# A second product made of seven, for the last 1024 tokens of a chunk-attention and ELU-FFN kernel

## The chip, the cores and the metric

The program runs on one core of one Trainium2 chip. The metric is device time in microseconds (us). The engines are TensorE (PE; its weight loads are listed apart as PEld), VectorE (DVE), ScalarE (ACT), GpSimd (POOL) and SyncE (SP), which issues the DMA transfers. The kernel before took 849.08 us, the median of three runs (848.92 to 850.63).

## The reference

```python
# q, k, v: 8 batches, 8 heads, 576 tokens, 64 features; chunks of 64 tokens
scores = 1/sqrt(64) * q_c @ k_c^T             # inside one chunk of 64 tokens
attn = exp(scores - max) ; attn = attn / (sum(attn) + 1e-9)
x = (attn @ v_c) -> 4608 tokens x 512         # heads side by side
h = x @ w_in                                  # 512 x 2048
g = where(h > 0, h, exp(min(h, 0)) - 1)       # ELU
out = g @ w_out                               # 2048 x 512, float32
```

The weights come as 64-bit floats, the rest as 32-bit floats.

## The kernel before

**Numbers.** Every operand of a large product is kept as a pair `hi`, `lo` of the rounded type float32r, whose sum is the float32 value. `three` (L405) makes one product of 128 x 128 by 128 x 512 from three matmuls: hi by hi, hi by lo, lo by hi. A split is a rounding copy on ACT (`hi`) and a subtraction on DVE or POOL (`lo`).

**Blocks.** The 4608 tokens are 9 blocks of 512. Three blocks are plain: for each of 16 slices f of the 2048 hidden features `hidden(f)` makes the slice of h from 4 `three`, `elu` and a split follow, and the slice goes into a queue of second products. The other six blocks form three superblocks of 1024 tokens (s = 0, 1, 2). There the first product is made by Winograd's form of Strassen's scheme: with weights and tokens cut in halves, a pair of slices (g = 0 to 7) for both token halves needs seven products of halves instead of eight. Their weight operands, among them four sums (S1 to S4), are made once, in the second plain block, by `combine` (L469: sums on POOL, split on ACT and DVE, written to `a_dram`), and loaded for each pair (`load_a`, 256 KB each, L531). The token operands T1 to T4 are made by `prepare` (L560). x_ps and y_ps are the two PSUM banks in which the products p1 to p7 add up; c1 to c4 (`keep`, L628) copy x_ps away on ACT, and d1 to d3 (`add`, L631) add y_ps to such a copy on DVE.

**Second product.** In all blocks before the change it is plain: `second_next` (L644) takes one item from the queue and makes one `three` of 128 tokens by 512 output columns, with w_out as the moving operand. 16 slices add up in four PSUM banks (o0 to o3), one for each 128 tokens. Results are copied to SBUF and stored in rows of 2 KB (`copy_out`, L446). The lo parts of w_out are loaded from `lo_dram` in a ring (`load_lo`, 512 KB for two slices, L546).

**Order.** PE, ACT, DVE and SP follow the source exactly; the order inside a block is written out in strings, one word for one step. POOL's order is chosen by the framework. One superblock is eight passes through PAIR and then the 16 lines of KEPT: in PAIR the first 512 tokens' h is used at once, while the other 512 tokens' is kept in `g_kept` and multiplied in KEPT. The words that matter here:

- p1 to p7, c1 to c4, d1 to d3 as above; Q is one item of the second product (three matmuls);
- 1, 2, 3, 4 are the next step of the pair's four ELU parts (1 and 3 end in a split and an entry in the queue, 2 and 4 in `g_kept`); 5 is 3 of the pair before;
- m, E, z, h, s, v, x, q, k, l, V are the attention of the tokens needed next: l issues eight q and k loads of 128 KB (sixteen of 64 KB where the 128 tokens lie in two batches), h ends with a DVE transpose, the ACT copy `unturned` (L369) and four small transfers `turned` on SP (L373), which the product v in the same pair needs;
- in KEPT, G splits the next kept slice.

As SP works in the order of the source, one pair's list on SP is: the weight load for p1 of the next pair after p1, then p2, p6, the four `turned` transfers, p5, the q and k loads, p7, p4, p3, and the v load; the lo load of w_out falls among the last.

Of the kernel before, what the change touches and what calls it, by code (L numbers as in the profile page):

```python
# [10 lines left out]
F32 = mybir.dt.float32  # L11
# [9 lines left out]
def kernel(  # L21
# [26 lines left out]
    P = 128  # L48
# [17 lines left out]

    first = ctx.enter_context(tc.tile_pool(name="first", bufs=1))
    sm = ctx.enter_context(tc.tile_pool(name="sm", bufs=4))
    stp = ctx.enter_context(tc.tile_pool(name="stp", bufs=3))
    fill = ctx.enter_context(tc.tile_pool(name="fill", bufs=1))  # L70
    const = ctx.enter_context(tc.tile_pool(name="const", bufs=1))
# [4 lines left out]
    ident = first.tile([P, P], F32, name="ident")  # L76
    fill.tile([P, 64], F32, name="unused")
    k_turned = const.tile([P, NK, P], F32, name="k_turned")
# [445 lines left out]
    def flat(t):  # L524
        return t.rearrange("p a b -> p (a b)")

    def a_place(i: int):

        return flat(weights[0][0])[:, i * 4 * P:(i + 1) * 4 * P]
# [114 lines left out]
    def second_next():  # L644
        if not queue:
            return
        (n0, o_ps, put), f, tt, hi, lo = queue.pop(0)
        ts = slice(tt * P, (tt + 1) * P)
# [8 lines left out]
        if not plain and tt == NTT - 1 and f % 2:  # L657
            uses.append(f)
            if len(uses) + RING <= NG * (1 + 2 * NS):
                load_lo((f - 1 + 2 * RING) % NF)  # L660

    RING = NG // 2
# [49 lines left out]
    def warm(n: int):  # L712
# [53 lines left out]
    SECOND_PAIR = (  # L766
        "p1 c1 5 5 h Q 4 p2 d1 4 Q q k p6 c2 1 Q Q 1 p5 1 1 Q l p7 c3 d2 Q Q 2 p4 c4 2 Q 3 p3 d3 "
        "3 3 3 s v x V"
    )
    PAIR = (  # L770
        "m p1 c1 4 E Q 4 z p2 d1 Q p6 c2 h 1 Q Q 1 p5 1 q k 1 Q l p7 c3 d2 Q Q 2 p4 c4 2 Q 3 p3 d3 "
        "3 3 3 s v x V"
    )
    KEPT = (
# [186 lines left out]
    def do(item: str):  # L961
        if item == "Q":
            second_next()
        elif item == "P":
            second_products()
# [32 lines left out]
    t3_place.append(late.tile([P, 2, 2 * TB], F32R, name="t3_place"))  # L998
    c11, c21 = [late.tile([P, TB], F32, name=name) for name in ("c11", "c21")]
    x_ps, y_ps = [ps_h.tile([P, TB], F32, name="h") for _ in range(2)]  # L1000

    pair = None
    for s in range(NS):
        n0 = (PLAIN + 2 * s) * TB
        run = n0, o_tiles(), a_half_place
        for g in range(NG):
            before, pair = pair, Pair(s * NG + g)
            for item in ((FIRST_PAIR, SECOND_PAIR)[g] if not s and g < 2 else PAIR).split():
                if item[0] == "p":
                    pair.product(int(item[1]))  # L1010
                elif item[0] == "c":
                    pair.keep(int(item[1]))
                elif item[0] == "d":
                    pair.add(int(item[1]))
                elif item in "45":
                    if before:
                        next(before.parts["3" if item == "5" else item], None)
                elif item in "123":
                    next(pair.parts[item])
                else:  # L1020
                    do(item)
        preparing, kept = s + 1 < NS, iter(range(NF))
        run = n0 + TB, o_tiles(), b_half_place
        for line in KEPT:
            for item in line.split():
                if item == "4":
                    next(pair.parts["4"], None)
                elif item == "G":
                    split_kept(next(kept))
                else:  # L1030
                    do(item)
    queue.sort(key=lambda item: item[2])
    while queue:
        second_next()

# [26 lines left out]
```

## Time and profile before

| | |
|---|---|
| median of three runs | 849.08 us |
| profiled execution: span, the time that the profile gives | 847.6 us |
| PE, PEld busy | 826.6, 674.8 us |
| DVE, ACT, POOL busy | 498.9, 484.4, 177.0 us |
| matmuls of the second product (`o`) | 1728 (416 x 3 + 320 + 160) |
| DMA | 164.10 MB, mean 194 GB/s |
| first, second and last superblock | about 331 to 505, 505 to 680 and 680 to 844 us |

All times are of one profiled execution. Rows of a timeline give start, length, engine, line, operation and what is written from what; in brackets the idle time before it and what ended it. "SPq" rows are DMA issues, whose length is SP's time and not the transfer's. A busy PE counts overlapping matmuls once.

### The profile page before, as it was taken

The numbers are of one execution on the slowest core, as the hardware profiler recorded it, in microseconds if no ns is written. First come the engines' busy times: TensorE is split into PE (matmuls) and PEld (weight loads), VectorE is DVE, ScalarE is ACT, GpSimd is POOL, SyncE is SP. The second block draws the span as 40 slices with busy tenths as digits, with TensorE's granted clock in tenths as the row PEclk, the third lists the DMA queues.
The fourth block names the chain that finished last, engine by engine and source line by source line (L and its number), as shares of the span: only waits on it lengthen the run. The fifth ranks groups of instructions, "written<-read, shape, count | busy, mean of one in ns | idle before, by whom it ended". The sixth has DMA issues, their size and how long they took to land.

```text
span 847.6 us, 15721 instructions
## 1 busy us (share of the span) xinstructions
PE 826.6 (98%) x5949; PEld 674.8 (80%) x5949; DVE 498.9 (59%) x717; ACT 484.4 (57%) x868; POOL 177.0 (21%) x150
## 2 busy tenths in 40 slices
PE   6799999999989999999999999999999999999998
PEld 5688777888768878888888888888887888888786
DVE  5898996656765678666565755666545333233411
ACT  6899885454444446755666436656664355555521
POOL 0000004255302111211113531111125211111120
PEclk9999999999999999999999999999999999999999
DMA  9856954766866785698898666789844365545231
GB/s 253 248 177 193 304 158 138 239 203 215 264 206 170 200 237 169 194 259 231 232 256 254 171 164 201 198 239 263 237 146 141 106 195 160 167 142 162 90 110 49
DMA packets 178795, 164.10 MB, mean 194 GB/s; under 512 B 65568, under 2 KB 161312, under 8 KB 178720
## 3 DMA queue, kind: packets, MB, share of 16 engines
q1 hardware_dynamic: 178720, 163.10, 65.5%
q8 instruction: 47, 0.77, 0.4%
q14 instruction: 28, 0.23, 0.1%
HBM read 131.07 MB, written 28.31 MB: 188 GB/s over the span
## 4 chain that ended last, share of the span: by engine, by line
PE 81%; issue 8%; DVE 3%; DMA 3%; ACT 2%; SPq 2%; POOL 2%; POOLq 0%; ACTq 0%; DVEq 0%
PE o L408 40%; PE h L408 36%; PE ps_a L235 2%; POOL glo L443 2%; PE ps_a L243 1%; DMA v_sb<-in_v_dram 1%; SPq L199 1%; PE h L425 1%; DMA st<-in_moe_w_out_dram 1%; PE ps_a L302 1%; DMA a_dram<-kept 0%; DVE g_kept L583 0%; SPq L114 0%; DMA kept<-in_k_dram 0%; PE ps_a L257 0%
## 5 line engine op out<-in xcount | busy, mean ns | idle before, releaser
L408 PE MATMUL o<-wo_hi,ghi 128*128 128x512 f32 x416 | 164.1, 395 | 0.3 <-ACT k_sb L448 0.3
L408 PE MATMUL o<-wo_hi,glo 128*128 128x512 f32 x416 | 162.7, 391 | 1.0 <-DVE glo L443 0.5
L408 PE MATMUL o<-wo_lo,ghi 128*128 128x512 f32 x416 | 162.1, 390 | 0.0
L590 POOL TENSOR_TENSOR glo<-e,ghi 128x512 fp32r<-128x512 f32 x46 | 59.6, 1295 | 310.2 <-ACT ghi L588 310.2
L408 PE MATMUL h<-xhi,wi_hi 128*128 128x512 f32 x324 | 108.0, 393 | 0.0
L408 PE MATMUL h<-xlo,wi_hi 128*128 128x512 f32 x324 | 106.7, 389 | 0.0
L408 PE MATMUL o<-wo_hi,wo_lo 128*128 128x512 f32 x320 | 99.8, 390 | 1.0 <-DVE kept L448 1.0
L408 PEld LDWEIGHTS o<-wo_hi,glo 128*128 128x128 f32 x416 | 78.1, 188 | 19.5 <-DVE glo L443 1.8
L408 PEld LDWEIGHTS o<-wo_hi,ghi 128*128 128x128 f32 x416 | 78.1, 188 | 17.6 <-ACT ghi L440 0.5
L408 PEld LDWEIGHTS o<-wo_lo,ghi 128*128 128x128 f32 x416 | 78.1, 188 | 15.8
L629 ACT COPY kept<-h 128x512 f32<-128x512 f32 x72 | 42.3, 588 | 60.8 <-PE h L408 60.7
L408 PE MATMUL h<-wi_lo,wi_hi 128*128 128x512 f32 x288 | 75.1, 396 | 0.0
L408 PE MATMUL h<-wo_lo,wi_hi 128*128 128x512 f32 x288 | 72.9, 389 | 0.0
L408 PEld LDWEIGHTS o<-wo_hi,wo_lo 128*128 128x128 f32 x320 | 60.1, 188 | 14.4 <-DVE kept L448 1.9
L408 PEld LDWEIGHTS h<-xhi,wi_hi 128*128 128x128 f32 x324 | 60.8, 188 | 13.0
L408 PEld LDWEIGHTS h<-xlo,wi_hi 128*128 128x128 f32 x324 | 60.8, 188 | 12.3
L408 PE MATMUL h<-xhi,wi_lo 128*128 128x512 f32 x180 | 70.2, 390 | 0.0
L583 DVE SCALAR_TENSOR_TENSOR g_kept<-e,g_kept 128x512 f32<-128x512 f32 x48 | 35.5, 739 | 57.2 <-ACT e L580 57.2
L633 DVE TENSOR_TENSOR g_kept<-h,kept 128x512 f32<-128x512 f32 x48 | 33.1, 689 | 51.6 <-ACT kept L629 27.2
L408 PEld LDWEIGHTS h<-wo_lo,wi_hi 128*128 128x128 f32 x288 | 54.0, 188 | 11.3
L580 ACT ACTIVATE e<-e 128x512 f32<-128x512 f32 x96 | 60.7, 633 | 3.1
L408 PE MATMUL o<-wo_lo 128*128 128x512 f32 x160 | 62.3, 389 | 0.0
(115 smaller groups left out, 1329.8 us busy)
## 6 DMA issues: line engine op xcount, KB each, us to landing
wi_hi<-a_dram SPq DMA_DIRECT2D x168, 256.0 KB, 3.7
wo_lo<-lo_dram SPq DMA_DIRECT2D x52, 512.0 KB, 4.8
kept<-in_q_dram SPq DMA_DIRECT2D x100, 128.0 KB, 3.7
kept<-in_k_dram SPq DMA_DIRECT2D x100, 128.0 KB, 4.1
st<-in_moe_w_in_dram SPq DMA_DIRECT2D x16, 512.0 KB, 4.5
st<-in_moe_w_out_dram SPq DMA_DIRECT2D x16, 512.0 KB, 4.9
v_sb<-in_v_dram SPq DMA_DIRECT2D x32, 256.0 KB, 6.0
a_dram<-kept SPq DMA_DIRECT2D x16, 512.0 KB, 4.0
```

What stands on the lines that cost most here:

```text
L199: nc.sync.dma_start(out=dst[p0:p0 + n], in_=src[b, :, s0:s0 + n, :].rearrange("h s d -> s h d"))
L235: nc.tensor.matmul(scores[halves[c], j, hp, :], lhsT=qT[halves[j], hp, halves[c]], rhs=kT[halves[j], hp, halves[c]], start=True, stop=True,)
L243: nc.tensor.matmul(x_ps[halves[j], c, hp, :], lhsT=v_sb[halves[c], 2 * hp + j, :], rhs=aT[halves[c], :, j * NK + hp], start=True, stop=True,)
L302: nc.tensor.matmul(turned_ps[half, h, :], lhsT=a[half, h, :], rhs=ident[half, half], start=True, stop=True,)
L408: nc.tensor.matmul(ps, lhsT=a, rhs=b, start=start, stop=stop, skip_group_check=onto)
L425: nc.tensor.matmul(h, lhsT=w[:, kt, :], rhs=x[:, kt, :], start=i == 0, stop=i == len(terms) - 1)
L443: engine.tensor_tensor(out=glo, in0=e, in1=ghi.bitcast(F32), op=ALU.subtract)
L580: nc.scalar.activation(out=e, in_=e, func=AF.Exp, scale=-1.0)
L583: nc.vector.scalar_tensor_tensor(out=to, in0=e, scalar=-1.0, in1=c, op0=ALU.add, op1=ALU.max)
L590: engine.tensor_tensor(out=lo, in0=e, in1=hi.bitcast(F32), op=ALU.subtract)
L629: nc.scalar.copy(out=c21 if i == 4 else self.kept[i - 1], in_=x_ps)
L633: nc.vector.tensor_tensor(out=to, in0=y_ps, in1=self.kept[kept], op=ALU.add)
```

## The change

For the last superblock (s = 2) the second product is made of seven products of halves, too, and turned round: the weights are the stationary operand, 512 tokens the moving one, and the result has output columns on the partitions and tokens along the row. BOPS are its seven weight operands: three quarters of w_out (A11, A12, A22) and four sums (S1 to S4).

- **Weight operands.** `Combination` makes the four sums of one of 16 units in seven steps, one for each word b (in SECOND_PAIR, PAIR and LAST_FIRST) or B (in KEPT of s = 1): load of lo into `quad`; one, two and two additions on POOL; rounding copy on ACT; subtraction on DVE; two writes to `b_dram`. `quad` is a single buffer. The word w at the end of PAIR writes one of twelve parts of the three quarters to `b_dram`, half of them from `lo_dram`. `load_b` loads one operand (256 KB) into a ring of eight.
- **Token operands.** In the last superblock all four ELU parts of a pair are kept (`kept_direct`, `raw_place`, `g_kept`). t1 to t4, th and tl make the sums T1 to T4 and T2's split on DVE and ACT; G (`turn_split`) makes a split for the products 5, 7, 4 and 3.
- **Order.** LAST_FIRST, LAST and LAST_LAST replace PAIR for s = 2, and TURNED replaces its KEPT stage. Products 1 and 2 are made in the pairs, the others in TURNED. The results add up in x2 and y2 (two banks each), are taken out by u (ACT copy), a (DVE addition) and s (`evacuate`: a DVE transpose of 32 x 32 squares, then four transfers with pieces of 128 bytes; for the last quarter two of the four are issued by ACT).
- KEPT's second word 4 stands two lines further down, POOL follows the source, three pools are put at the other end of SBUF, and an unused tile is gone.

```diff
-    first = ctx.enter_context(tc.tile_pool(name="first", bufs=1))
...
+    first = ctx.enter_context(tc.tile_pool(name="first", bufs=1, side="right"))
...
+    class Combination:
...
+        def load(self):
+            nc.sync.dma_start(out=quad, in_=self.lo)
...
+        def combine(self):
+            a11, a21, a12, a22 = [quad[:, i] for i in range(4)]
+            self.pool(quad, self.hi, quad, ALU.add)
+            yield
+            self.pool(a22, a21, a22, ALU.add)
+            self.pool(a21, a11, a21, ALU.subtract)
+            yield
+            self.pool(a11, a22, a11, ALU.subtract)
+            self.pool(a12, a12, a11, ALU.subtract)
+
+        def cast(self):
+            nc.scalar.copy(out=quad_hi(), in_=flat(quad))
...
+    def combinations():
+        for n in range(NG * NM):
+            unit = Combination(n)
+            unit.load()
+            yield
+            yield from unit.combine()
+            yield
+            for step in (unit.cast, unit.subtract, unit.write):
+                step()
+                yield
+
+    def load_b(j: int):
+        i, g = b_order[j]
+        nc.sync.dma_start(
+            out=weights[0][3][:, j % (NF // 2), :].bitcast(F32),
+            in_=b_dram[g, :, BOPS.index(PRODUCTS[i][0])].rearrange("p l d -> p (l d)"))
+
+    def b_product(i: int, g: int, m: int, hi, lo):
...
+        three((y2 if i in (2, 5, 3) else x2)[m], ah, al, hi, lo, first, True, onto=not first)
+        if m == NM - 1 and j + NF // 2 < len(b_order):
+            load_b(j + NF // 2)
...
     PAIR = (
-        "m p1 c1 4 E Q 4 z p2 d1 Q p6 c2 h 1 Q Q 1 p5 1 q k 1 Q l p7 c3 d2 Q Q 2 p4 c4 2 Q 3 p3 d3 "
-        "3 3 3 s v x V"
+        "b b b m p1 c1 4 E Q 4 z p2 d1 Q p6 c2 b h b 1 Q Q 1 p5 1 q k 1 b Q l p7 c3 d2 Q Q b 2 p4 c4 "
+        "2 Q 3 p3 d3 3 3 3 s v x V w"
+    )
+    LAST_FIRST = (
+        "b b b p1 c1 Q Q p2 d1 Q Q b b b p6 1 c2 Q p5 1 1 1 Q p7 c3 d2 Q Q 2 p4 c4 2 3 p3 d3"
+    )
+    LAST = (
+        "5 4 p1 c1 Q 5 p2 4 t1 d1 Q 5 p6 1 t2 c2 p5 1 t3 1 1 th tl t4 p7 c3 d2 Q Q 2 p4 c4 2 3 p3 "
+        "d3"
+    )
...
+    TURNED = (
+        "6 Y Z 6 Y Z t1 6 Y t2 t3 th tl t4 Q Q 6 a10 s10 a11 s11 G 6 G 6 G 6 G 6 5 G u20 u21 5 G "
+        "5 G 5 G 5 G 5 G 5 G 5 G 7 G 7 G 7 G 7 G 7 G 7 G 7 G 7 u30 u31 G 5 G a30 a31 4 G 4 G s30 s31 "
+        "3 G 3 G 3 G 3 G 3 G 3 G 3 G 3 G a20 s20 a21 s21 G G W0 s40 W1 s41"
     )
     KEPT = (
-        "4 m G E 4 Q Q Q Q G",
+        "4 m G E Q Q Q Q G",
         "Q Q Q Q G z",
-        "Q Q h Q Q G l",
+        "Q Q h Q Q G 4 l",
         "Q Q xB11 q k Q Q G",
-        "Q Q xB21 Q Q G",
-        "Q Q Q Q s v x V G",
-        "Q Q m xt1 Q Q E G",
+        "Q Q xB21 Q Q G B",
+        "Q Q Q Q s v x V G B",
+        "Q Q m xt1 Q Q E G B",
...
     ctx.enter_context(tc.manual_schedule(engines={
         mybir.EngineType.PE, mybir.EngineType.Activation, mybir.EngineType.DVE,
-        mybir.EngineType.SP,
+        mybir.EngineType.SP, mybir.EngineType.Pool,
     }))
...
+    def evacuate(item: str):
...
+            nc.vector.transpose(out=to, in_=src)
+            t0, d0 = n0 + th * TB, dh * HALF + m * P
+            for i in range(P // Q):
+                (nc.scalar if which == 4 and i % 2 else nc.sync).dma_start(
+                    out=out[t0:t0 + TB, d0 + i * Q:d0 + (i + 1) * Q].rearrange(
+                        "(j t) d -> t j d", t=Q),
+                    in_=to[i * Q:(i + 1) * Q].rearrange("p (j d) -> p j d", d=Q))
```

More of the change, by code (lines that the diff above doesn't have):

```diff
@@ L999 @@
     c11, c21 = [late.tile([P, TB], F32, name=name) for name in ("c11", "c21")]
-    x_ps, y_ps = [ps_h.tile([P, TB], F32, name="h") for _ in range(2)]
-    pair = None
+    quad = late.tile([P, 4, P], F32, name="quad")
+    k_flat = flat(k_turned)
+    combinations_next = combinations()
+    direct_writes = iter([(half, name, lo) for half in range(2) for name in DIRECT for lo in range(2)])
+    turned_order = [item for item in TURNED.split() if item in "65743"]
+    turned_order += ["4"] * (NG - turned_order.count("4"))
@@ new lines, in turn_split @@
+    def turn_split(splits, ready):
+        i, g = next((i, g) for i, g in splits if i != 6)
+        n = len(ready)
+        ring = flat((weights[1][3], weights[0][1])[n // 4 % 2])
+        hi, lo = [ring[:, (2 * (n % 4) + j) * TB:(2 * (n % 4) + j + 1) * TB] for j in range(2)]
+        src = {5: raw_place(0, g), 4: raw_place(1, g), 7: g_place(2 * g), 3: g_place(2 * g + 1)}[i]
+        nc.scalar.copy(out=hi, in_=src)
+        nc.vector.tensor_tensor(out=lo, in0=src, in1=hi.bitcast(F32), op=ALU.subtract)
+        ready[i, g] = hi, lo
@@ new lines, with pair_step @@
+    pair = None
+    def pair_step(item: str, before):
+        if item[0] == "p":
+            pair.product(int(item[1]))
+        elif item[0] == "c":
+            pair.keep(int(item[1]))
+        elif item[0] == "d":
+            pair.add(int(item[1]))
+        elif item in "45":
+            if before:
+                next(before.parts["3" if item == "5" else item], None)
+        elif item in "123":
+            next(pair.parts[item])
+        elif item[0] == "t":
+            before.combine(item[1])
+        elif item == "w":
+            for what in [next(direct_writes, None)]:
+                if what:
+                    write_direct(*what)
+        else:
+            return False
+        return True
@@ L1003 @@
     for s in range(NS):
         n0 = (PLAIN + 2 * s) * TB
+        last = s == NS - 1
         run = n0, o_tiles(), a_half_place
+        if last:
+            x2, y2 = run[1][:NM], run[1][NM:]
         for g in range(NG):
             before, pair = pair, Pair(s * NG + g)
[L1008 to L1020, printed above, removed]
+            order = PAIR
+            if last:
+                order = LAST_FIRST if g == 0 else LAST_LAST if g == NG - 1 else LAST
+            elif not s and g < 2:
+                order = (FIRST_PAIR, SECOND_PAIR)[g]
+            for item in order.split():
+                if item[0] == "u":
+                    evacuate(item)
+                elif not pair_step(item, before):
```

153 lines of the change are left out of this document (139 added, 14 removed), and 5 rows, old and new, of tables (KEPT, TURNED).

## The prediction

> **What bounds the kernel now.** I read the engine totals first, then busy time by stage, then the chain of waits, then the timeline of one pair.
>
> ```profile
> PE 826.6 (98%) x5949; PEld 674.8 (80%) x5949; DVE 498.9 (59%) x717; ACT 484.4 (57%) x868; POOL 177.0 (21%) x150
> ```
>
> The stages, in a table of stretches (length, then busy us and instructions of PE, PEld, DVE, ACT, POOL; granted clock; DMA share; GB/s): the pairs of the first superblock, of the second, and of the last.
>
> ```profile
> 362.50:460.00 97.50, 97.50 (x781) 79.86 (x780) 60.65 (x95) 60.69 (x105) 16.51 (x13) 1.00 0.86 243
> 516.20:614.00 97.80, 97.77 (x781) 80.06 (x780) 60.43 (x96) 59.59 (x102) 15.54 (x12) 1.00 0.81 226
> 687.76:777.52 89.76, 89.76 (x398) 74.33 (x397) 29.08 (x44) 50.34 (x85) 15.52 (x12) 1.00 0.55 165
> ```
>
> TensorE never rests there, at full clock, and ACT and DVE are idle for 37 of 97.5 us in the first two. Only a change in the number of matmuls, or a new stall, moves the time. A matmul is shown as 390 ns long but they overlap; its price is its spacing, read from one unbroken piece of the chain (start, us, what):
>
> ```profile
> 800.69 43.15 PE o L408 x189
> ```
>
> 43.15 / 189 = 0.228 us. In the first two superblocks the DMA engines are over 80% busy, and the SP queue works through one list in order; that is where the new weight sums are put.
>
> **What is taken away.** The second product of the last 1024 tokens has 16 weight slices x 8 token tiles x 3 = 384 matmuls of 512 columns. After, it has 7 products x 8 slices x 2 halves of columns x 3 = 336. 48 x 0.228 = **-10.9 us**, all on the path. Two stalls go too:
>
> ```profile
> 636.47 0.50 PE L408 MATMUL o<-wo_hi,wo_lo 128*128 128x512 f32 x1 [0.35 <-DVE kept L448]
> 800.69 0.50 PE L408 MATMUL o<-wo_hi,wo_lo 128*128 128x512 f32 x1 [0.67 <-DVE kept L448]
> ```
>
> Both waited for a copy out of PSUM on DVE behind an elu step of L583; the second step `4` now comes two lines later in KEPT, and the last KEPT stage is gone: **-1.0** (bounds -1.0 and 0).
>
> **What is added, and its cover.** In the last superblock DVE gets t1 to t4 and a split per pair: 4 elu steps, 3 adds, 2 splits, 5 new = 14 x 0.69 = 9.7 us; ACT 8 activations at about the cast's 0.62, 4 copies of 0.59 (411.68, below) and 3 casts = 9.2:
>
> ```profile
> L583 DVE SCALAR_TENSOR_TENSOR e<-e,c 128x512 f32<-128x512 f32 x48 | 33.0, 687 | 48.0 <-ACT e L580 48.0
> L588 ACT CAST ghi<-e 128x512 fp32r<-128x512 f32 x48 | 29.8, 621 | 50.9 <-DVE e L583 41.0 <-PE h L408 9.8
> ```
>
> TensorE has 54 matmuls = 12.3 us per such pair, which covers both: 0, and at most 8 x 0.4 = 3 if c2 or c3 slips. Making GpSimd's order that of the source costs 0: its timeline already runs in source order. The same goes for pools on the other side: no instruction changes.
>
> **The weight sums** are the term that decides. One unit is: a 256 KB load to `quad`, five GpSimd adds, a cast on ACT, a subtraction on DVE, two 256 KB writes; each PAIR runs one unit, starting with the adds and ending with the load for the next pair. PAIR also issues `w`, a 512 KB write. On its queue the load stands behind the whole list of SP. That list in a pair of the first superblock (start, length, what):
>
> ```profile
> 397.48 2.47 SPq L373 DMA_DIRECT2D turned<-unturned  x4
> 400.05 0.58 SPq L533 DMA_DIRECT2D wi_hi<-a_dram  x1
> 400.67 2.02 SPq L215 DMA_DIRECT2D kept<-in_q_dram  x4
> 402.74 1.85 SPq L215 DMA_DIRECT2D kept<-in_k_dram  x4
> 404.69 1.23 SPq L533 DMA_DIRECT2D wi_hi<-a_dram  x2
> ```
>
> These are h, p5, l, then p7 and p4. The two writes come between p5 and l, the load between p7 and p4. p7's load ends at 405.3 (half of 1.23); two writes at 0.34 (a store's issue, row below) to 0.58 (a load's), taken as 0.4 with its gap, put the new load at 406.1. Its landing: a 256 KB load issued at this very spot (first row, stretch 404.6 to 405.2) against the quiet last superblock (690 to 780).
>
> ```profile
> wi_hi<-a_dram SPq DMA_DIRECT2D x1, 256.0 KB, 4.4
> ...
> wi_hi<-a_dram SPq DMA_DIRECT2D x43, 256.0 KB, 3.1
> ```
>
> I take 4.4, the same place with the same traffic ahead: 410.5. The adds, by GpSimd's present ones on 512 and 256 columns:
>
> ```profile
> 158.16 2.55 POOL L473 TENSOR_TENSOR kept<-wi_hi,wi_lo 128x512 f32<-128x512 f32 x2 [15.13 <-DVE glo L443]
> 160.79 2.94 POOL L473 TENSOR_TENSOR kept<-kept 128x256 f32<-128x256 f32 x4
> ```
>
> 1.275 for 512 columns and 0.735 for 256, so by the line through them 0.465 for 128; 1.275 + 4 x 0.465 and a gap = 3.25: done at 413.8. Then the cast, 0.62 (L588), to 414.45. On ACT, in order, the cast stands behind c2 and ahead of what follows in the next pair:
>
> ```profile
> 411.68 0.59 ACT L629 COPY kept<-h 128x512 f32<-128x512 f32 x1 [1.81 <-PE h L408]
> 413.12 0.62 ACT L369 COPY unturned<-turned 128x512 f32<-128x512 f32 x1 [0.85 <-DVE turned L366]
> 413.76 2.48 SPq L373 DMA_DIRECT2D turned<-unturned  x4
> 415.03 0.69 DVE L583 SCALAR_TENSOR_TENSOR e<-e,c 128x512 f32<-128x512 f32 x1 [1.95 <-ACT e L580]
> 416.44 0.59 ACT L629 COPY kept<-h 128x512 f32<-128x512 f32 x1
> 417.60 1.52 PE L408 MATMUL h<-xhi,wi_hi 128*128 128x512 f32 x6
> ```
>
> There was a hole of 0.85 us for it after c2, but it ends 1.35 us after `unturned` was due at 413.12. `unturned`, two activations, a cast and c3 (416.44) all move by 1.35; c3 frees x_ps for p4 (417.60) and has 417.60 - 417.03 = 0.57 to spare. So TensorE waits. And it is a **loop**: `unturned` releases the four `turned` transfers on SP, behind which stand the writes, l, and the next load. Its length is 2.57 + 0.62 + 0.8 + 4.0 + 0.6 (SP) + 4.4 (landing) + 3.25 (adds) + 0.65 (cast) + 0.65 (`unturned`) = about 17.6 us against the pair's 16.28 (413.76 - 397.48): **+1.35 us per pair**, not absorbed but added each time. It holds where SP has q and k loads to issue. (`w` falls after l and V, and SP has time left before it waits for `unturned` again: 0 to 0.5. The DVE subtraction, 0.7, stands behind `unturned`'s transpose, where DVE waits 1.95 us for ACT (415.03): 0. The one unit in KEPT, spread over eight lines, and that in LAST_FIRST have no loop: 0 to 1.) The first link of each superblock is worse, as the pair before it has twice as many of them:
>
> ```profile
> 360.25 0.55 SPq L549 DMA_DIRECT2D wo_lo<-lo_dram  x1
> 364.27 0.62 ACT L369 COPY unturned<-turned 128x512 f32<-128x512 f32 x1 [0.85 <-DMA wo_lo<-lo_dram]
> ...
> 526.92 3.88 SPq L215 DMA_DIRECT2D kept<-in_q_dram  x8
> 530.84 4.41 SPq L215 DMA_DIRECT2D kept<-in_k_dram  x8
> 535.35 1.23 SPq L533 DMA_DIRECT2D wi_hi<-a_dram  x2
> 539.35 0.62 ACT L369 COPY unturned<-turned 128x512 f32<-128x512 f32 x1 [0.85 <-DVE turned L366]
> ...
> 608.04 3.33 SPq L533 DMA_DIRECT2D wi_hi<-a_dram  x3
> ```
>
> First superblock: in SECOND_PAIR the load stands behind the one at 360.25 and goes at 360.85, + 4.4 + 3.25 + 0.65 = 369.15, allowed 364.27 + 0.57: 4.3. Second: p7's load ends at 535.95, + 0.8 + 4.4 + 3.25 + 0.65 = 545.1, allowed 539.92: 5.2. Then five pairs in the first and four in the second (at 608.04 the product loads follow at once, no q or k load is left) at 1.35: 4.3 + 5.2 + 9 x 1.35 = **+21.7 us**. From below it is 0 (the load in time); from above, with the landing at 5.5 instead of 4.4 (the writes and `w` are new traffic), 11 x 1.1 more = 34.
>
> **The end.** Each quarter of the output now leaves as 4096 pieces of 128 bytes. The end before, a store's issue (332/344/383 ns), and DMA packets with their share of 16 engines' time in 0.7 to 10 us (nearly all of 256 bytes) and 690 to 780 us (nearly all of 1 KB):
>
> ```profile
> 843.43 0.39 PE L408 MATMUL o<-wo_hi,wo_lo 128*128 128x512 f32 x1
> 843.86 0.69 DVE L448 COPY g_kept<-o 128x512 f32<-128x512 f32 x1 [1.96 <-PE o L408]
> ...
> L449 SPq DMA_DIRECT2D out_dram<-g_kept x16: 332/344/383, 333.1 to 844.6; - x16
> ...
> q1 hardware_dynamic: 6719, 2.09, 91.1%
> ...
> q1 hardware_dynamic: 12479, 14.61, 54.9%
> ```
>
> 90 x 16 x 0.549 / 12479 = 63 ns a packet, 55 for 1 KB; 9.3 x 16 x 0.911 = 136 us, less 512 of 55 ns, over the other 6207 = 17 ns for 256 bytes. No row has 128-byte stores: from 9 (half) to 55 (a 1 KB packet); I take 17, the nearest size. The last two quarters, 8192 pieces, start to leave about 1.7 us after the last product 3 (an add, a transpose and an issue), and 36 matmuls = 8.2 us follow that product; 512 per engine x 17 = 8.7 us, so the queue is nearly dry by the last transpose (a DVE pass like the copy's 0.69), and the tail is the 3.8 us of before (843.8 to 847.6) plus one more issue and some backlog: **+2** (+0.4 at 9 ns; at 55 it ends 1.7 + 28.2 + 1 - 8.2 = 22.7 after TensorE, +19). Earlier quarters compete with the weight loads (256 KB per 6 matmuls = 1.37 us); the ring is 7 products = 9.6 us ahead, against 4.4 landing and 4.4 of stores: **+1** (0 to 18).
>
> The Trainium skill (DMA: Bandwidth & Descriptors, Specifications) puts the smallest transfer at line rate at 512 bytes, with a read-modify-write below; that speaks against this output, but the 256-byte loads here ran at 224 GB/s, and no run here shows such stores.
>
> **The sum**: 847.6 - 10.9 - 1.0 + 21.7 + 2 + 1 = 860.4 of span. The median shown is 849.08, 1.5 above the span; so **862 us**.
>
> **Rivals.** *The load is in time*, 840 us: without the loop, 860.4 - 21.7 = 838.7, + 1.5. For it: TensorE is the bound now, and a landing under 3.05 us closes the loop; against: 3.1 is the quiet landing. *It is only a little late, or throughput binds instead of latency*, 848: at 3.1 the loop adds 9 x 0.05 + 3.0 + 3.9 = 7.4; by throughput a pair moves 3.8 + 1.3 = 5.1 MB, and the best ten microseconds gave 303 GB/s, so 16.8 us per pair, 14 x 0.5 = 7.
>
> ```profile
> DMA packets 13175, 11.15 MB, mean 232 GB/s; under 512 B 4069, under 2 KB 12851, under 8 KB 13171
> ...
> 10.00:20.00 10.00, 5.58 (x144) 4.66 (x144) 8.50 (x19) 8.18 (x26) 0.00 (x0) 1.00 1.04 303
> ```
>
> (11.15 MB in 394 to 442 is 3.8 a pair.) *Small stores cost double*, 34 ns, without the loop: 512 x 34 = 17.4, a tail of 1.7 + 17.4 + 1 - 8.2 = 11.9 instead of 3.8, +8, and two earlier bursts each 8.7 + 4.4 - 9.6 = 3.5 late: 838.7 - 3 + 8 + 7 + 1.5 = 852, slower; it decides from about 30 ns. By the rule of the Trainium skill named above the time would be this one.
>
> **Chances.** The loop 0.48 (own range 853 to 872, landing 3.6 to 5.5), load in time 0.31, in between 0.13, small stores 0.08. About 0.2% (1.7 us) can be told from no change: slower 0.48 + 0.08 + 0.05 = 0.61, the same 0.07 (0.04 of the between, 0.03 of a load in time with a worse tail), faster 0.32. The range must reach the in-time case: 839 to 871.
>
> **What would show it.** ACT's cast waiting for GpSimd's adds and these for `quad`'s load, for 2 us or more in each pair; pairs of 17 to 18.5 us instead of 16.28 in the first two superblocks, TensorE idle before p4; 12.3 us for a last pair; a tail near 6 us. I am wrong if `quad` lands before the pair's first product, or if TensorE stays full from 362 to 614 us.

## The result and the profile after

After the change the kernel takes 887.33 us (median of five runs, 883.31 to 888.12) beside 850.24 us for the kernel before on the same chip (848.92 to 851.41): a ratio of 1.0439, 95% interval 1.0413 to 1.0466. It is **slower by 37 us**; 862 was predicted. The profiled executions have spans of 881.2 and 847.6 us; the one after is the shortest of its five, so that the differences read from the traces add up to 33.6 us and not to 37.

The first part of the page after, its engine totals:

```profile
PE 831.8 (94%) x5901; PEld 674.4 (77%) x5901; DVE 567.4 (64%) x820; ACT 506.4 (57%) x910; POOL 208.8 (24%) x209
```

TensorE has its 48 matmuls fewer (5901 instead of 5949) and is busy for longer. The table of stretches (length, then busy us and instructions of PE, PEld, DVE, ACT, POOL; granted clock; DMA share; GB/s) says where: pairs of the first superblock, of the second, of the last.

```profile
360.00:478.00 118.00, 101.23 (x757) 80.30 (x755) 61.06 (x96) 58.98 (x102) 33.33 (x41) 0.91 0.91 248
553.00:660.00 107.00, 93.32 (x726) 73.81 (x725) 55.98 (x88) 54.09 (x95) 28.57 (x35) 0.92 0.88 246
732.17:817.85 85.68, 85.68 (x379) 70.95 (x378) 63.80 (x99) 62.34 (x106) 0.00 (x0) 1.00 0.63 188
```

In the pairs that carry a sum, TensorE rests for 13 to 14% of the time and its granted clock falls from 1.00 to 0.91; in the last superblock it is full. The length of a pair is read from one copy that each has, `c4` on ACT. In the changed kernel's timeline of ACT:

```profile
394.59 0.57 ACT L747 COPY c<-h 128x512 f32<-128x512 f32 x1
414.98 0.59 ACT L747 COPY c<-h 128x512 f32<-128x512 f32 x1 [0.42 <-PE h L406]
433.71 0.57 ACT L747 COPY c<-h 128x512 f32<-128x512 f32 x1
```

and in that of the kernel before:

```profile
403.15 0.57 ACT L629 COPY c<-h 128x512 f32<-128x512 f32 x1
419.43 0.57 ACT L629 COPY c<-h 128x512 f32<-128x512 f32 x1
435.72 0.57 ACT L629 COPY c<-h 128x512 f32<-128x512 f32 x1
```

20.39 and 18.73 us instead of 16.28 and 16.29. Cutting each span at these copies, and doing so for some of the experiments below too, gives one table (us; "pairs" is from the first c4 of a superblock to its eighth, "kept" from there to the next superblock's first, "rest" from the last superblock's first to the end of the span):

| kernel | start | pairs 1 | kept 1 | pairs 2 | kept 2 | rest | span |
|---|---|---|---|---|---|---|---|
| before | 338.9 | 113.1 | 61.2 | 114.0 | 60.3 | 160.2 | 847.6 |
| after | 336.2 | 137.9 | 62.3 | 135.8 | 59.9 | 149.0 | 881.2 |
| no_sums | 338.8 | 113.0 | 61.2 | 115.9 | 60.0 | 149.0 | 837.9 |
| engines_only | 337.7 | 123.1 | 61.3 | 115.6 | 60.0 | 149.2 | 846.8 |
| traffic_only | 338.5 | 125.4 | 69.1 | 130.8 | 60.0 | 149.0 | 872.9 |
| small_transfers | 341.9 | 113.0 | 61.2 | 115.5 | 60.0 | 149.2 | 840.8 |
| two_quads | 339.4 | 127.9 | 68.0 | 130.6 | 60.0 | 149.3 | 875.2 |
| sums_in_gaps_2 | 338.5 | 113.3 | 62.3 | 115.0 | 64.9 | 149.0 | 843.0 |

From before to after: -2.7 at the start (the kernels of the table lie between 336.2 and 341.9 there), **+24.9 and +21.8 in the pairs with a sum**, +1.1 and -0.4 in the kept blocks, -11.1 in the rest (-12.0 to the last matmul, +0.8 of tail), together +33.6.

One pair of the first superblock after, from one issue of `turned` to the next, out of the timeline (some rows of SP, GpSimd, ACT and TensorE):

```profile
408.88 2.47 SPq L371 DMA_DIRECT2D turned<-unturned  x4
412.08 0.60 SPq L581 DMA_DIRECT2D b_dram<-wi_hi  x1
413.27 2.33 SPq L213 DMA_DIRECT2D kept<-in_q_dram  x4
415.64 1.85 SPq L213 DMA_DIRECT2D kept<-in_k_dram  x4
418.22 0.60 SPq L556 DMA_DIRECT2D quad<-lo_dram  x1
...
423.08 1.67 POOL L559 TENSOR_TENSOR quad<-wo_hi,quad 128x512 f32<-128x512 f32 x1 [1.28 <-DMA quad<-lo_dram]
424.83 2.09 POOL L559 TENSOR_TENSOR quad<-quad 128x128 f32<-128x128 f32 x4
426.95 0.62 ACT L572 CAST wi_hi<-quad 128x512 fp32r<-128x512 f32 x1 [1.18 <-POOL quad L559]
427.47 0.62 ACT L367 COPY unturned<-turned 128x512 f32<-128x512 f32 x1
428.12 1.84 SPq L371 DMA_DIRECT2D turned<-unturned  x3
```

This is the predicted loop, link for link, but of 428.12 - 408.88 = 19.24 us instead of 17.6: 9.34 on SP up to the load (8.6 predicted), 4.86 from there to the adds (4.4; 4.8 to 6.4 in other pairs), 3.87 for the adds with their gaps (3.25), and 1.17 for cast and `unturned` (1.3). Behind the cast wait `unturned`, c3 and then TensorE. The waits of the whole run (total, times, longest):

```profile
POOL quad L559 <- DMA quad<-lo_dram: 48.8, 13, 8.9
...
PE h L406 <- ACT kept L747: 24.9, 9, 7.2
```

TensorE behind such a wait, and later in the same pair, from its timeline:

```profile
412.02 2.93 PE L406 MATMUL h<-xhi,wi_hi 128*128 128x512 f32 x6 [3.30 <-ACT kept L747]
...
421.58 1.52 PE L406 MATMUL h<-wi_lo,wi_hi 128*128 128x512 f32 x6
```

After 3.30 us of rest six matmuls take 2.93 us, where six take 1.52 later in the pair: such a stall is paid a second time, by 1.4 us in these six. So far all speaks for the loop, only longer. The experiments say that it is the smaller part.

### The profile page after: what moved, and what is told of

It reads as the page before. It is cut to its first block, busy times and chain, and to the rows that moved or that the text cites. A ratio compares the mean times of both kernels' runs of the same rounds, so it can differ in the third digit from the quotient of the medians.

```text
span 881.2 us, 16030 instructions
## 1 busy us (share of the span) xinstructions
PE 831.8 (94%) x5901; PEld 674.4 (77%) x5901; DVE 567.4 (64%) x820; ACT 506.4 (57%) x910; POOL 208.8 (24%) x209
## 3 DMA queue, kind: packets, MB, share of 16 engines
q10 hardware_dynamic: 2112, 0.26, 0.2%
## 4 chain that ended last, share of the span: by engine, by line
PE 63%; DMA 11%; issue 9%; SPq 6%; ACT 5%; DVE 3%; POOL 3%; ACTq 0%; POOLq 0%
PE o L406 32%; PE h L406 27%; DMA b_dram<-lo_dram 3%; DMA quad<-lo_dram 2%; DMA wi_hi<-a_dram 2%; SPq L213 2%; POOL glo L441 2%; PE ps_a L233 1%; DMA b_dram<-wo_hi 1%; SPq L197 1%; PE ps_a L241 1%; POOL quad L559 1%; SPq L625 1%; DMA v_sb<-in_v_dram 1%; ACT unturned L367 1%
## 5 line engine op out<-in xcount | busy, mean ns | idle before, releaser
L406 PE MATMUL h<-xhi,wi_hi 128*128 128x512 f32 x324 | 116.3, 422 | 30.5 <-ACT kept L747 24.9
L406 PE MATMUL o<-wo_hi,ghi 128*128 128x512 f32 x352 | 140.8, 400 | 0.3 <-ACT k_sb L446 0.3
L406 PE MATMUL o<-wo_hi,glo 128*128 128x512 f32 x352 | 139.1, 395 | 1.1 <-DVE glo L441 0.6
L406 PE MATMUL o<-wo_lo,ghi 128*128 128x512 f32 x352 | 138.8, 394 | 0.0
L406 PEld LDWEIGHTS h<-xhi,wi_hi 128*128 128x128 f32 x324 | 63.8, 200 | 48.6 <-ACT kept L747 35.1
L682 POOL TENSOR_TENSOR glo<-e,ghi 128x512 fp32r<-128x512 f32 x32 | 41.4, 1293 | 167.8 <-ACT ghi L680 167.8
L406 PEld LDWEIGHTS o<-wo_hi,glo 128*128 128x128 f32 x352 | 67.1, 191 | 17.1 <-DVE glo L441 1.6
L406 PEld LDWEIGHTS o<-wo_hi,ghi 128*128 128x128 f32 x352 | 67.0, 190 | 15.2 <-ACT k_sb L446 0.4
L406 PEld LDWEIGHTS o<-wo_lo,ghi 128*128 128x128 f32 x352 | 67.1, 191 | 13.6
L406 PE MATMUL o<-wo_hi,wo_lo 128*128 128x512 f32 x240 | 71.0, 390 | 0.0
L406 PEld LDWEIGHTS h<-wi_lo,wi_hi 128*128 128x128 f32 x288 | 52.9, 188 | 11.6 <-DVE g_kept L751 0.3
L406 PE MATMUL o<-wo_lo 128*128 128x512 f32 x192 | 59.9, 389 | 0.0
```

The lines of the kernel that those rows point to most:

```text
L406: nc.tensor.matmul(ps, lhsT=a, rhs=b, start=start, stop=stop, skip_group_check=onto)
L682: engine.tensor_tensor(out=lo, in0=e, in1=hi.bitcast(F32), op=ALU.subtract)
```

## The experiments

**Theory A** is that of the prediction: a loop of latencies through SP's list, the landing of `quad`, GpSimd's adds and the cast on ACT ahead of `unturned`. **Theory B**: the bytes. A pair moves about 248 GB/s x 19.4 us = 4.8 MB after, and 243 x 16.3 = 4.0 before, with the DMA engines 0.91 busy in place of 0.86. Later came **C** (GpSimd's and DVE's own work) and **S** (the number of SP's issues).

### The cast moved out of the way: sums_late_cast, and the load ahead of q and k: load_before_qk

```diff
-        "b b b m p1 c1 4 E Q 4 z p2 d1 Q p6 c2 b h b 1 Q Q 1 p5 1 q k 1 b Q l p7 c3 d2 Q Q b 2 p4 c4 "
-        "2 Q 3 p3 d3 3 3 3 s v x V w"
+        "m p1 c1 4 E Q 4 z p2 d1 Q b p6 c2 h 1 Q Q 1 p5 1 q k 1 b b b Q l p7 c3 d2 Q Q 2 p4 c4 "
+        "2 Q 3 p3 d3 3 3 b 3 b s v x V w b"
```

(SECOND_PAIR loses its b, LAST_FIRST has four after d2.)

load_before_qk instead moves one b, the load, from behind p7 to right behind the writes:

```diff
-        ... 1 q k 1 b Q l p7 c3 d2 Q Q b 2 p4 c4 "
+        ... 1 q k 1 b b Q l p7 c3 d2 Q Q 2 p4 c4 "
```

> The same work in another order: in PAIR the load of a unit is issued ahead of p6 and so ahead of the q and k loads, the adds follow the pair's first glo on GpSimd, and the cast on ACT stands behind h, c3, c4 and d3 at the end of the pair; only then the subtraction and, in the end, the writes. The cast no longer stands ahead of the copy `unturned`. Theory A (a loop through SP's list, the load's landing, the adds, the cast and `unturned` sets the pair): the pairs of the first two superblocks fall from 19 to 20 us back to 16.3 to 16.8, and the time from 887 to 838 to 846 us. Theory B (the pair's transfers, 5.1 MB, and SP's list are simply too much for 16.3 us, in any order): pairs stay above 18 us and the time above 870.

> One word moved: the load of the next unit is issued right behind the two writes and ahead of the q and k loads; the cast stays ahead of `unturned`. Theory A: the loop loses the q and k loads' issue (4.2 us) and p7's load, and gains the wait for the writes to land (about 3); with a shorter landing (4 instead of 5.8) it gets 2 to 3 us shorter, so the pairs take 16.5 to 17.5 and the time is 855 to 868 us. Theory B: the same traffic, and SP now waits for a landing in the middle of its list: no better than 887.

Measured: 900.24 us, ratio 1.0614 (1.0595 to 1.0633), and 898.33 us, 1.0587 (1.0559 to 1.0614). Both are worse than the change itself. In sums_late_cast the waits of TensorE have moved:

```profile
PE ps_a L241 <- DMA turned<-unturned: 34.2, 18, 6.2
```

The cast no longer holds up `unturned`, but SP issues `turned` late instead: with one `quad`, the load stands behind the landing of the write, and `turned` behind the load. From the timeline of SP in that run:

```profile
400.21 1.60 SPq L581 DMA_DIRECT2D b_dram<-wi_hi  x1
401.90 1.40 SPq L581 DMA_DIRECT2D b_dram<-quad  x1
403.39 1.21 SPq L625 DMA_DIRECT2D wi_hi<-a_dram  x2
407.09 0.36 SPq L556 DMA_DIRECT2D quad<-lo_dram  x1
407.55 0.52 SPq L625 DMA_DIRECT2D wi_hi<-a_dram  x1
408.16 1.84 SPq L371 DMA_DIRECT2D turned<-unturned  x3
```

So neither run cut the loop; they closed another one through SP, and A was not refuted by them, nor B shown.

### w out of the pairs: parts_in_kept; GpSimd's order left to the framework: pool_by_framework

```diff
-        "2 Q 3 p3 d3 3 3 3 s v x V w"
+        "2 Q 3 p3 d3 3 3 3 s v x V"
```

with one w in twelve lines of the first kept block; and, in the other run, alone:

```diff
-        mybir.EngineType.SP, mybir.EngineType.Pool,
+        mybir.EngineType.SP,
```

> The twelve 512 KB writes w are moved out of PAIR into twelve lines of the first superblock's KEPT stage. Theory A: w stands behind the load on SP and is not a link of the loop, it only slows the load's landing (5.8 with it, 4.4 predicted without): 12 links shorter by 1 to 1.5 us, 870 to 877 us. Theory B: a tenth of the bytes of a pair less, and 0.8 to 2.3 us of SP's time: pairs of 17.5, about 860.

> One part undone: GpSimd's order is again left to the framework. Prediction as on record: costs and brings nothing, so the time is that of the changed kernel within 3 us, 884 to 890. A rival: the framework's order lets a glo pass the adds that wait for `quad`, and the time falls by more than 5 us.

Measured: 884.85 us, 1.0428 (1.0400 to 1.0456), not to be told from the change itself: the pairs last 138.2 and 135.7 us, as with w in them, and the kept block takes the twelve 512 KB copies for nothing (62.3 us in both). And 893.47 us, 1.0529 (1.0507 to 1.0551): the source's order on GpSimd is worth **6 us** to this kernel. They are lost in the second kept block, 65.8 us instead of 59.9, where the framework put a sum's adds ahead of `glo` while `quad` had not landed (its timeline of GpSimd):

```profile
682.71 1.64 POOL L559 TENSOR_TENSOR quad<-wo_hi,quad 128x512 f32<-128x512 f32 x1 [7.87 <-DMA quad<-lo_dram]
```

### What the sums cost, and which part of them: no_sums, engines_only, traffic_only, small_transfers

Of the change, the four alter the sums alone (and w, which no_sums and small_transfers have in the first kept block); in all but traffic_only products 3 to 7 load direct parts of the weights in place of the sums. In no_sums b and B do nothing:

```diff
         elif item == "b":
-            next(combinations_next, None)
+            pass
```

In engines_only, write() is empty and load() is

```diff
-            nc.sync.dma_start(out=quad, in_=self.lo)
+            if self.g == self.m == 0:
+                nc.sync.dma_start(out=quad, in_=self.lo)
```

In traffic_only:

```diff
     def combine(self):
-        a11, a21, a12, a22 = [quad[:, i] for i in range(4)]
-        self.pool(quad, self.hi, quad, ALU.add)
...
+        yield
+        yield
     def cast(self):
-        nc.scalar.copy(out=quad_hi(), in_=flat(quad))
+        pass
...
-        for lo, src in enumerate((quad_hi().bitcast(F32), flat(quad))):
+        for lo, src in enumerate((flat(quad), flat(quad))):
```

In small_transfers, on top of that:

```diff
-        nc.sync.dma_start(out=quad, in_=self.lo)
+        nc.sync.dma_start(out=quad[:8], in_=self.lo[:8])
```

and the same for the two writes and w.

> Leaves out the weight sums altogether: no sum is formed or written, the direct copies go out in the kept block of the first superblock, and products 3 to 7 take direct parts of the weights in place of the sums, so their output is not that of the reference. What is left is the gain of the seven products alone. All theories: 887.3 - 46.6 = 840.7, about 838 to 842, pairs of the first two superblocks back at 16.3 us. If it stays above 850, something outside the sums is paid for that I have not seen.

> Keeps the five adds, the cast and the subtraction of every sum, and leaves out their transfers: quad is loaded once at the start and never again, nothing of it is written, and products 3 to 7 take direct parts in place of the sums, so the output is not that of the reference; w stays. Theory A: without the landing the loop is open, 16.3 to 16.7 us a pair, 840 to 846. Theory B: the traffic is gone, the same 840 to 846. A third theory C (the port that GpSimd shares with DVE, or ACT's and DVE's own work, slows the pairs): 17.5 us and more a pair, above 860.

> Keeps every transfer of the weight sums (the load to quad, two writes, w) where it is in the lists, and leaves out the five adds, the cast and the subtraction; both writes send what was loaded, so products 3 to 7 use wrong weights. Theory A (a loop: SP's list, the load's landing, the adds, the cast, and behind it on ACT the copy unturned that frees the next transfers of SP): without the cast the loop is open, pairs fall to 16.3 to 16.9 us, 842 to 850. Theory B (the DMA engines: 4.8 MB a pair instead of 3.95, at 245 GB/s in both, 91% busy): nothing changes, pairs stay at 18 to 20 us, 875 to 888.

> As traffic_only (no adds, cast or subtraction; 872.6 us), but the load to quad, its two writes and w in the pairs move only 8 of the 128 partitions: the same number of issues at the same places of SP's list, one sixteenth of the bytes. The direct copies go out whole in the kept block of the first superblock; products 3 to 7 take direct parts in place of the sums, so the output is not that of the reference. Theory B (bytes: the DMA engines are full, 0.96 of them in traffic_only): pairs back at 16.3 to 16.6 us, 839 to 845. Theory S (issues: SP's list of one pair was 14.7 of 16.28 us before, and four more issues of about 0.65 us with their gaps make it over 17): pairs stay at 17.3 us and more, 858 to 872.

Measured, with the median, its ratio to before and interval, and the difference to no_sums:

| kernel | us | ratio | over no_sums |
|---|---|---|---|
| no_sums | 838.72 | 0.9891 (0.9860 to 0.9921) | |
| small_transfers | 842.64 | 0.9923 (0.9902 to 0.9944) | 3.9 |
| engines_only | 851.98 | 1.0048 (1.0032 to 1.0063) | 13.3 |
| traffic_only | 872.57 | 1.0290 (1.0249 to 1.0331) | 33.9 |
| after | 887.33 | 1.0439 (1.0413 to 1.0466) | 48.6 |

**The seven products by themselves are a gain of 9.8 us.** The adds, casts and subtractions cost little: in the table above engines_only loses 10.1 us to no_sums in the pairs of the first superblock and nothing after (8.9 between the spans; the medians lie 13.3 apart, as the profiled execution is the fastest of eight). 8.7 of that is one pair, 25.21 us instead of 16.54, in which the single load that this kernel has left lands late. C falls. The transfers alone, with no add or cast waiting for `quad`, cost 33.9: A had said 842 to 850. And the same issues with a sixteenth of the bytes cost nothing in the pairs (113.0 and 115.5 beside 113.0 and 115.9; the 3 us of difference between the spans lie ahead of the first pair): S falls, **the bytes carry it** (or the number of packets, which falls with them here). How they do it shows in SP's list: the three product loads ahead of `turned`, and `turned`, from small_transfers' timeline of SP

```profile
428.81 2.94 SPq L617 DMA_DIRECT2D wi_hi<-a_dram  x3
432.95 2.48 SPq L371 DMA_DIRECT2D turned<-unturned  x4
```

and from traffic_only's timeline, with ACT's `unturned` between them:

```profile
439.88 4.56 SPq L617 DMA_DIRECT2D wi_hi<-a_dram  x3
440.04 0.62 ACT L367 COPY unturned<-turned 128x512 f32<-128x512 f32 x1
444.54 2.47 SPq L371 DMA_DIRECT2D turned<-unturned  x4
```

In the first SP is done at 431.8 and waits 1.2 us for `unturned`. In the second it never rests from 425.2 to 447, its issues take longer (q and k up to 2.45 and 3.16 where they took 1.74 and 1.85), and `turned` is issued 3.9 us after `unturned` was there; the product with v waits for it, the first of TensorE's waits in traffic_only:

```profile
PE ps_a L241 <- DMA turned<-unturned: 18.4, 11, 2.7
```

`turned` also lands later, in 3.1 us instead of the 1.9 of the changed kernel (medians). By the table, the pairs of traffic_only take 27.3 us longer than those of no_sums, and its first kept block 7.9 (69.1 beside 61.2). In that block two products with v wait for `turned`, the first by

```profile
468.64 1.01 PE L241 MATMUL ps_a<-turned,v_sb 64*64 64x64 f32 x32 [2.33 <-DMA turned<-unturned]
```

and the matmuls behind both waits are slow, at a granted clock of 0.89 from 464 to 496 us. What makes an issue longer the trace doesn't show; that it goes with the bytes under way, the pair of runs does.

### The loop cut: two_quads, and the transfers on another queue: sums_on_act_queue

```diff
-    quad = late.tile([P, 4, P], F32, name="quad")
+    quads = [late.tile([P, 4, P], F32, name="quad"),
+             kept_st[2][:, 3 * TB:4 * TB].rearrange("p (i c) -> p i c", i=4)]
...
+    elif item == "r":
+        next(loads).load()
```

An item r issues the load of the sum after next where b issued that of the next. sums_on_act_queue has in addition, and likewise for the two writes and w:

```diff
-            nc.sync.dma_start(out=self.quad, in_=self.lo)
+            nc.scalar.dma_start(out=self.quad, in_=self.lo)
```

> Everything is computed. quad gets a second buffer (a part of kept that is unused in the pairs), and each load is issued one pair earlier than in the changed kernel, so it has a whole pair to land; adds, cast, subtraction, writes and w stand where they were. Theory A: the cast never waits, the first links go too, pairs 16.3 to 17 us, 843 to 855. Theory B: the bytes are the same, pairs stay at 18 to 20 us, 875 to 888.

> Everything is computed. As two_quads (877.4 us), but the load to quad, its two writes and w are issued by ACT on its own queue: the same bytes, and SP's list is as long as before the change. Theory S: pairs fall to 16.3 to 16.9 us, 845 to 858 with the first link's 9 us still there. Theory B: the bytes are the same, pairs stay at 17.5 to 20 us, 870 to 885; more if the issues hold up ACT's copies.

Measured: 877.43 us, 1.0335 (1.0295 to 1.0376), and 909.21 us, 1.0707 (1.0684 to 1.0730). With the loop cut, pairs of 16.31 and 16.34 us appear in the first superblock, but also 20.14, and 20.8 and 22.0 in the second: 10 us are won of 48.6, B's outcome. The first link, 25.23 us, is still there, as the first load stands where it stood. TensorE's first wait is then that for `turned`, 13.8 us in 8 waits. On ACT's queue the time is longer still, but that run is no clean test of queue or issues, since it brings waits of its own. The cast's result lies in `wi_hi`, the tile of the product loads, and those loads, on SP, now wait for its write, on ACT's queue, to land:

```profile
SPq L623 <- DMA b_dram<-wi_hi: 56.6, 10, 6.3
```

two_quads has no such wait. ACT, too, stands for the landing of a write ahead of the load into the same buffer (29.0 us in 11 waits). TensorE then waits for `turned` (27.4 us in 15 waits) and for the product loads (11.7 in 4).

### The same bytes elsewhere: sums_elsewhere, sums_in_gaps, sums_in_gaps_2

All three keep two_quads' second buffer and take the sums out of most pairs. SUMS lists what a kept block adds to each of its lines; the last kernel has

```diff
+    SUMS = (
+        {1: "w", 2: "w", 3: "r", 4: "w", 5: "w r", 6: "w", 7: "w", 8: "b b", 9: "b w", 10: "b b b", 12: "w"},
+        {1: "b b", 2: "b", 3: "b b b r", 4: "w", 5: "r", 6: "b b w", 7: "b", 8: "b b b w", 9: "b b",
+         10: "b r", 11: "b b b w", 12: "b b r", 13: "b", 14: "b b b"},
+    )
...
+    LAST = (
+        "b b b 5 4 p1 c1 Q 5 p2 4 t1 d1 Q 5 p6 r 1 t2 c2 p5 1 t3 1 1 th tl t4 p7 c3 b d2 b Q Q 2 p4 "
+        "b c4 2 3 p3 d3"
+    )
```

and three sums in pairs 1, 7 and 8 of the second superblock. sums_elsewhere had four sums in the first kept block, five in the second, one in each of the last pairs but the eighth, and six w in each kept block:

```diff
+        {1: "w", 2: "w", 3: "w r", 4: "w r", 5: "w b b b", 6: "w b b", 7: "b r b b b", 8: "b b",
+         9: "b r b b b", 10: "b b", 11: "b b b b", 12: "b b", 13: "b"},
```

and sums_in_gaps one in SECOND_PAIR, three in pairs 1, 2 and 8 of the second superblock, four in its kept block, eight in the last pairs:

```diff
+        {1: "w", 2: "w", 3: "w", 4: "w", 5: "w", 6: "w", 7: "w", 8: "w", 9: "w", 11: "w", 12: "w",
+         13: "w r", 14: "r"},
+        {1: "b b b", 2: "b b", 3: "b r", 6: "r b b b", 7: "b b", 8: "b", 9: "b b b", 10: "r b b", 11: "b",
+         13: "r b b b", 14: "b b", 15: "b"},
```

> Everything is computed. The sixteen sums leave the pairs of the first two superblocks: 4 are made in the kept block of the first, 5 in that of the second, 7 in the pairs of the last superblock (with the second buffer for quad); the direct copies go out in the two kept blocks. Theories B and S agree: the pairs are those of no_sums, 16.3 us, and the places that take the work have room (DMA share 0.53 in the second kept block and 0.65 in the last pairs of no_sums, GpSimd idle in the last): 838.7 to 845. The first kept block is the risk: its DMA share was 1.02 in no_sums with twelve copies of 0.5 MB, and is about the same with six copies and four sums; if it waits, up to 8 us more, 853.

> Everything is computed. The sums stand where the trace of no_sums showed the DMA engines below 0.8 and GpSimd with nothing urgent behind: one in the second pair of the first superblock, three in the pairs 1, 2 and 8 of the second, four in its kept block, eight in the pairs of the last; all twelve direct copies in the first kept block; each load at least half a pair ahead of its adds (two buffers for quad), and in the kept block the adds stand in GpSimd's order only after the load has had 12 us or more. Theory B with the reading of sums_elsewhere (its loss is GpSimd's glo standing behind adds that wait for quad's landing): no_sums' 838.7 plus about 1 for the pair 8 (16.9 instead of 16.0 in two_quads), 0 to 2 in the last pairs, 0 to 2 in the kept block: 840 to 844, faster than before. If the bytes hurt wherever they stand, the kept block and the last pairs stretch again as in sums_elsewhere: 855 and more.

> Everything is computed. As sums_in_gaps (853.95 us), with the places where its trace still showed TensorE idle changed: the first loads of the second superblock stood last in a full queue of SP (issued at 503.0, adds at 510.9, then 5.9 us of TensorE), so they are issued some 30 us earlier; four of the twelve direct copies go to the second kept block; no sum in pair 2 of either superblock, where a table of q and k loads already fills the DMA engines (22.1 us instead of 18.6), but one in the first kept block and one in pair 7; and GpSimd's adds are put one or two to a line of the kept block, so that a glo waits for less. If the bytes cost only where they meet a full stretch (B, read by place): 838.7 + 0.8 + 0.8 (pairs 7 and 8) + 1 + 1 (kept blocks) = about 842, 840 to 846. If they cost wherever they stand (about 0.9 us for each of the sixteen, as sums_in_gaps has over no_sums): 850 to 855.

Measured: 875.01 us, 1.0299 (1.0281 to 1.0318); 853.95 us, 1.0060 (1.0042 to 1.0077); and **845.28 us, 0.9958 (0.9944 to 0.9972)**, 3.3 us below the kernel before: a small gain, whose interval leaves out 1. In the first, the pairs are 16.28 us at once, but the kept blocks take 80.2 and 74.4 us, as GpSimd's adds waited there for `quad` with `glo` queued behind (waits of that run):

```profile
POOL quad L560 <- DMA quad<-lo_dram: 21.2, 4, 8.3
...
PE o L406 <- POOL wo_lo L680: 10.6, 5, 3.7
PE o L406 <- POOL glo L680: 10.1, 4, 3.6
```

In sums_in_gaps the first kept block still took 68.4 (a load issued last in a full list) and one pair 22.1. With those mended, the stretches of sums_in_gaps_2, cut at its own c4, are: pairs of the first superblock without a sum, first kept block, second kept block, pairs of the last superblock.

```profile
360.00:451.79 91.79, 91.79 (x697) 75.21 (x695) 57.16 (x91) 54.93 (x95) 14.29 (x11) 1.00 0.91 240
451.79:514.07 62.28, 61.49 (x388) 50.32 (x387) 39.61 (x43) 29.98 (x51) 33.50 (x26) 1.00 0.99 282
629.06:693.95 64.89, 61.88 (x294) 50.58 (x293) 35.85 (x30) 29.47 (x48) 47.19 (x43) 0.97 0.74 224
693.95:779.62 85.67, 85.67 (x379) 70.95 (x378) 71.08 (x105) 65.26 (x113) 24.93 (x33) 1.00 0.86 257
```

The sums and their bytes cost nothing in the last pairs (row 4: TensorE full) and 1.1 us in the first kept block (row 2: eight w and a sum). The 4.9 us of the second (row 3) are no price of the bytes: TensorE waits there once, for a `glo` that stood behind five adds, with GpSimd at work throughout:

```profile
674.04 3.96 POOL L560 TENSOR_TENSOR kept<-kept 128x128 f32<-128x128 f32 x4
677.96 2.24 POOL L680 TENSOR_TENSOR glo<-g_kept,ghi 128x512 fp32r<-128x512 f32 x1
...
680.26 0.79 PE L406 MATMUL o<-wo_hi,glo 128*128 128x512 f32 x1 [3.01 <-POOL glo L680]
```

So the bytes cost by place, not by amount. And rows 1 and 2 have TensorE full or nearly so at a DMA share of 0.91 and 0.99, beside 0.91 in the pairs of the changed kernel with TensorE at 86%: **the share of the DMA engines doesn't tell a harmless stretch from a harmful one**. What tells, by the waits of these runs, is whether something that TensorE will soon need stands behind the transfers.

## Why the prediction was wrong

**Right**, by its steps:
- 48 matmuls less and the two stalls: -10.9 and -1.0 were predicted, and from the last superblock's first c4 to the last matmul the trace has 876.6 - 732.2 = 144.4 us in place of 843.8 - 687.4 = 156.4: -12.0 (one of the two stalls, 0.35 us, lay in the second kept block, which is 0.4 shorter). A last pair is 12.24 us (12.3 predicted):

```profile
732.17 0.59 ACT L747 COPY c<-h 128x512 f32<-128x512 f32 x1
744.41 0.59 ACT L747 COPY c<-h 128x512 f32<-128x512 f32 x1
```

- DVE's and ACT's new work in the last pairs: 0 was predicted, and TensorE is full there.
- The loop exists, in the named place, with the named waits.

**Wrong, the step "The weight sums": +21.7 us**, where the trace has +24.9 and +21.8, 46.7 together. By its terms, the first links were put at 4.3 and 5.2 us and measured 8.5 and 6.9; the nine pairs behind them were put at 1.35 us each, 12.2, and lost 31.6, 3.5 each. Two errors lie in it.

First, its terms were too small. The pairs of the loop last 18.2 to 20.5 us instead of 17.6; in the pair shown above the excess is spread over SP's list, the landing and the adds, and in the others the landing is up to 6.4, above the bound of 5.5. The first link took 25.05 us instead of 16.56: the load landed 7.6 us after its issue, not 4.4, and the matmuls behind the stall ran at half pace:

```profile
358.07 0.42 SPq L556 DMA_DIRECT2D quad<-lo_dram  x1
...
365.67 1.27 POOL L559 TENSOR_TENSOR quad<-wo_hi,quad 128x512 f32<-128x512 f32 x1 [8.94 <-DMA quad<-lo_dram]
369.09 0.62 ACT L572 CAST wi_hi<-quad 128x512 fp32r<-128x512 f32 x1 [8.40 <-POOL quad L559]
...
373.39 2.93 PE L406 MATMUL h<-xhi,wi_hi 128*128 128x512 f32 x6 [7.20 <-ACT kept L747]
```

4.3 and these two, 3.2 for the landing and 1.4 for the slow matmuls, make 8.9, near the 8.5 measured. That a restart is slow was in no term. In the first link of the second superblock TensorE waits 5.53 us, and for a product load, not for a copy behind the cast.

Second, and larger, **the transfers were left out of the sum**: they were made a rival of the loop, of which one would bind, and priced at 7 us. Alone they cost 33.9 us. The adds, the cast and their waits bring 14.7 on top (887.3 - 872.6; 8.3 between the two profiled spans), and the two first links, which traffic_only doesn't have, are as large as that. In the nine pairs where the loop was forecast to bind, the changed kernel loses 31.6 us and traffic_only 27.5, and 7.9 more in the kept block behind: there the loop brings little that the transfers don't cost by themselves. The 7 us were 14 pairs of 0.5, by the best ten microseconds of the trace, 303 GB/s. The prediction's own rows had a better price: 243 GB/s at a share of 0.86 and 226 at 0.81 are 283 and 279 at a full share, and traffic_only, at 261 and 0.94 in the pairs, has 278:

```profile
387.00:452.00 65.00, 58.41 (x470) 46.77 (x469) 32.83 (x52) 33.11 (x57) 8.54 (x7) 0.95 0.94 261
```

With 280 the same formula gives 5.1 MB / 0.280 = 18.2 us a pair, 14 x 1.9 = 27 us, the size of the 27.3 that the pairs of traffic_only lose. That is an estimate and partly luck: it has nothing for the kept block, and the rate at a full share is no constant (240 GB/s at 0.91 in row 1 of sums_in_gaps_2 is 264). That the transfers alone would stop TensorE through one late small transfer, `turned`, was in no rival.

Smaller ones: **GpSimd's order at 0** was 6 us to the good (pool_by_framework). **The end at +2** was +0.8, and earlier bursts at +1 were 0. One pair of the second superblock takes 18.59 us in no_sums, where it took 16.62 before, and TensorE waits 1.5 us for `turned` in it, with no sum in the kernel; the cause wasn't looked for. The stores of 128 bytes are cheap, from the last 21 us of the changed kernel (queue of ACT: packets, MB, share; then KB and us to landing):

```profile
q10 hardware_dynamic: 2112, 0.26, 7.7%
...
out_dram<-c ACTq DMA_DIRECT2D x4, 64.0 KB, 2.2
```

21.2 us x 16 x 0.077 / 2112 = 12.4 ns a packet, between the 9 and the 17 of the prediction. The rival of small stores at double cost, which decided from 30 ns, falls. The Trainium skill (DMA: Bandwidth & Descriptors, Specifications) has the line rate from 512 bytes up and a read-modify-write below. The trace agrees with a lower rate, 128 bytes in 12.4 ns being 10 GB/s of one engine beside 19 for the prediction's 1 KB in 55 ns; a doubled time for a packet doesn't show. The rival "load in time", 840, was the time of the products without the sums: no_sums has 838.7, and two_quads shows that a load in time alone doesn't give it.

**What stays open**: why an issue of SP takes longer with more bytes under way, and whether it is bytes or packets that count. And whether `turned`, 32 KB a piece, would be in time if it didn't stand in the same list: it wasn't tried alone, and it lands later, too.

## What to carry to other kernels

When work is put into a stretch in which DMA is busy, count its transfers and not only its chain of latencies: here the transfers alone cost 33.9 of 48.6 us, and cutting the chain that the waits named returned a fifth. A first estimate of their price is their bytes by the rate that this stretch has today, over its DMA share; the best rate of the trace made it four times too cheap. A high DMA share is harmless where nothing behind it is due soon (the kept block of no_sums took twelve copies of 512 KB at 1.02 for nothing) and costly where a small, urgent transfer shares the list. New traffic belongs in the stretches whose next transfers are far ahead of their use, each load well ahead of the engine that consumes it, and no engine's in-order list should hold a wait for a landing ahead of work that TensorE needs.

## What the runs showed of the hardware

- After a rest of 3.30 us or of 7.20 us, six 512-column matmuls took 2.93 us instead of 1.52; after rests of 1.93 and 2.12 us they took 1.67 and 2.36. The granted clocks of the two stretches were 0.91 and 0.92. By the Trainium skill (TensorE: Matmul & The Clock Gate, Part 1) the array falls to half its clock after an idle window of about 3.4 us. The factor of 1.9 agrees; the length doesn't quite, as 3.30 us had the whole effect here and 2.12 us a part.
- A 128-byte store costs 12.4 ns of one DMA engine, and 64 KB of them land in 1.9 to 2.2 us.
- GpSimd's five adds took 3.76 us (1.67 + 2.09) in the pair shown and 3.32 (1.27 + 2.05) in the first link.
- One issue of SP took 0.3 to 0.6 us in most rows; w took 2.33 in a pair of the changed kernel, and 3.58 in the kept block of no_sums, at a DMA share of 1.02.
